# A rewritten opening and another order of products at chunk ends in a Fourier-mixing kernel with a gated feed-forward network

## The chip, the core and the metric

The kernel runs on one core of one Trainium2 chip. The core has five engines that run side by side, each working through its own list of instructions in order: TensorE (PE, matrix products; its weight loads are shown as PEld), VectorE (DVE), ScalarE (ACT), GpSimd (POOL) and SyncE (SP, which here only issues DMA transfers). They wait for each other through semaphores. The metric is the device time of one execution in microseconds; lower is better.

## The reference

`A_x` holds 8192 tokens of 448 numbers. Each token is normalised (`xn`, mean and variance over its 448 numbers). Two branches start from `xn` and meet at the end:

```python
xn = _layernorm(x, axis=-1)
s = _A_ref(xn, ...)          # rfft over the tokens, two complex block products
                             # (4 blocks of 112) with a relu between, soft threshold, irfft
g = _silu(_B_ref(xn, ...))   # (gelu(xn @ w_gate) * (xn @ w_up)) @ w_down, 448 -> 1792 -> 448
return x + s * g
```

Everything the change touches lies in the B branch, in the normalisation and in the first stage of the Fourier transform of the first tokens.

## The kernel before, in words

**Numbers.** Products are made in float16 pairs: a float32 operand is split into a high and a low float16 part, and three products (high by high, low by high, high by low) stand for one. So every weight and every token has a high and a low part to be made: ACT makes the high part (a cast or a scaled copy), DVE or POOL subtracts it from the original for the low one. Weights are first scaled by a power of two that comes from the largest magnitude in a block. That maximum is taken in three steps (`largest`, L442): DVE reduces along the rows, PE turns the column of maxima into a row by a product with a float32 identity (`identf`), DVE reduces again, PE spreads the result over all partitions, and DVE makes the scales (`scales`, L648).

**Tiling.** Tokens are taken as 64 tiles of 128 (4 tiles a chunk, 16 chunks; chunks 0 and 1 are special). The 1792 columns of the hidden layer are 14 blocks of 128, called f. The first pass (p=0) does f=0 to 7 for all chunks and stores partial sums; the second pass (p=1) does f=8 to 13, adds the partial sums, applies the silu, multiplies by the Fourier branch and stores the output. Chunks 0 and 1 of the first pass use plain products (`plain`, L1153): for each f, 22 matmuls of 512 columns, of gate and up together (for chunk 0, f=0 alone, they are done in two halves of 256 columns, tiles 0 and 2 first, then 1 and 3). From chunk 2 on, pairs of tiles and pairs of blocks are multiplied by a scheme with seven products in place of eight (`unit`, L1025, products 1 to 7 named a1 to a7), with combinations of weights (`gu_comb`, L731) and of tokens prepared beforehand. The token combinations are written to DRAM (`xts`) and read back transposed into `xta` and `xtb` (`xt_load`, L976).

**Phases.** Phase 1 normalises the tokens chunk by chunk and runs the first Fourier stage (`stage1`, L565); phase 2 does the block products of the Fourier branch; phase 3 the last Fourier stage. They are laid beside the feed-forward products, which run on PE from beginning to end.

**Order.** The order of instructions on each engine is made when the program is built, by a planner (`Pace`, L49). It keeps a planned time for every engine, ring buffer and DMA. Each part of the work is a Python generator; `yield` hands control to whichever task is due next, `yield ev(...)` waits in planned time for another task's `done(...)`. Operations are appended to their engine's list in the order in which the planner reaches them. On the chip there is no planner: the engines run their lists and wait on semaphores only for real data. Starts of later phases are tied to fixed planned times (`T1`, `DT`, `END1` to `END3`). `Either` (L204, called `B`) gives an operation to DVE or POOL, whichever ends first by plan. All instructions of the helper carry line L199 in the profile, so tiles tell them apart: `x` and `st` (tokens, statistics), `xs` (their float16 parts), `xta` (the transposed tokens of chunk 0, later the transposed combinations), `wst` (raw gate and up weights), `wt` (their float16 parts), `fx`, `fh`, `fe`, `fc` (maxima and scales), `dw` (down weights), `bx`, `by`, `bd`, `bf` (PSUM banks, two each).

**The opening** (`begin`, L1915) is written out by hand. It issues the loads of the four tiles of chunk 0 on SP's queue and of the first weight block and the identity on ACT's. Tile 0's mean and variance are made by DVE, those of tiles 2, 1 and 3 by ACT with two accumulating passes. POOL takes the power -0.5 and DVE refines it in four small operations (`rsqrt`, L518). DVE normalises (`normal`), ACT casts the high part, POOL (tile 0) or DVE (tile 2) subtracts for the low part, PE transposes both (`turn`, L1883), and DVE and ACT copy the transposed parts out of PSUM into `xta`. Then the first half of f=0 can start. Tiles 1 and 3 go the same way behind it (`token`, L1890), and stage 1 of all four tiles after that. `weights` (L2050) meanwhile starts the loads of the next blocks, `gu_block` (L662) takes their maxima and scales, and `gu_split` (L712) makes their parts; four buffers `wst` hold raw blocks. `down_weights` (L754) takes the maxima of the down weights, `begin1` (L2024) does the statistics and tokens of chunk 1, `gu_combs` (L700) the combinations for chunks 2 and on.

**A chunk end in the first pass** (`chunk`, L1441): after the last unit's products a3 and a7, the down products (`down`, L1364; for one tile 8 blocks x 3 matmuls of 448 columns) are made in the order tile 0 (f=0 to 5), the unit's last product a4, tile 1 (f=0 to 5), tile 0 and tile 1 (f=6, 7), tile 2, tile 3. Then the next chunk starts with its a1.

Of the kernel before, what the change touches and what calls it, by code (L numbers as in the profile page):

```python
# [24 lines left out]
PL = 2  # L25
# [23 lines left out]
class Pace:  # L49
# [4 lines left out]
    def __init__(self):  # L54
        self.now, self.last, self.n, self.heap = 0.0, 0.0, 0, []
        self.free, self.seen, self.dma = {}, {}, 0.0
        self.port = {"DVE": [], "POOL": []}
# [74 lines left out]
    def issue(self, e, op, out, ins, run):  # L132
        outs, ins, start = self.start(e, out, ins)
        if e == "SP":
# [33 lines left out]
    def cost(self, e, op, start, out, ins):  # L168
# [8 lines left out]
        if e == "POOL":  # L177
            t = 1.1 if n < 8 and op == "tensor_tensor_pow" else 0.2 + 0.0023 * n
        elif n < 32:
            return 0.17  # L180
        elif psum or sb < 2 and op != "tensor_scalar":
            return 0.14 + 0.00107 * (n + 60 * (extra > 0))
# [191 lines left out]
def afno_geglu_kernel(ctx, tc, x, gu, wd, mlp, b1, b2, c_m, c_mt, c_small, out):  # L374
# [81 lines left out]

    EV = {}
# [46 lines left out]
    def stats(c):  # L504
# [157 lines left out]
    def gu_block(b, to):  # L662

        f0, n = BLK[b]
        for i in range(n):
            yield ev("wl", f0 + i, 0)
            t = EV["wst", f0 + i, 0]
            V.tensor_reduce(fm[:, i, :, b], t[:, 0:8].rearrange("p (i k) f -> p i (k f)", i=2),
                            axis=AXIS.X, op=ALU.max, apply_absolute_value=True)
            yield  # L670
        mx = fx[:, :, b]
        if n == 2:
            V.tensor_tensor(mx, fm[:, 0, :, b], fm[:, 1, :, b], op=ALU.max)
        else:
            V.tensor_copy(mx, fm[:, 0, :, b])
        yield
# [3 lines left out]
        scales_of_products(b, to)  # L680
        done("scales", b)
        for i in range(n):
# [7 lines left out]
            done("w", f)  # L690
# [9 lines left out]
    def gu_combs(fs):  # L700
# [3 lines left out]
        for f in fs:  # L704
            yield ev("wl", f, 1)
            yield from gu_comb(f, EV["wst", f, 1], wt[f][:, :, 8:16])
# [5 lines left out]
    def gu_split(f, t, d, k):  # L712
        if 0 < f < PF[0][1]:
# [4 lines left out]
            yield  # L718
# [6 lines left out]
        yield  # L725
        V.scalar_tensor_tensor(d[:, 1, 0:4 - k], t[:, k:4], scale(f, 0), d[:, 0, 0:4 - k],
# [4 lines left out]
    def gu_comb(f, t, d):  # L731

        c = yield from CB.get()
# [16 lines left out]
        CB.put(c)  # L750
# [3 lines left out]
    def down_weights(p):  # L754
# [398 lines left out]
    def plain(c, f):  # L1153
# [5 lines left out]
        for q, tk in enumerate((slice(0, 256), slice(256, 512)) if (c, f) == (0, 0) else (slice(0, 512),)):  # L1159
# [3 lines left out]
            for p, v in ((u, 0), (g, 4)):  # L1163
                for t in range(3):
                    T.matmul(p[:, tk], w[:, 0, v + t], xT[t][:, tk], start=t == 0 and tk.start == 0, stop=False,
                             skip_group_check=True)
                    T.matmul(p[:, tk], w[:, 0, v + t], xT[4 + t][:, tk], start=False, stop=False,
                             skip_group_check=True)
                    T.matmul(p[:, tk], w[:, 1, v + t], xT[t][:, tk], start=False, stop=False,
                             skip_group_check=True)  # L1170
                    yield pe()
                T.matmul(p[:, tk], w[:, 0, v + 3], xT[3][:, tk], start=False, stop=False, skip_group_check=True)
                T.matmul(p[:, tk], w[:, 1, v + 3], xT[3][:, tk], start=False, stop=tk.stop == 512,
                         skip_group_check=True)
# [218 lines left out]
    def ffn():  # L1393
# [34 lines left out]
        rings = (BD, BD, BX, BX)  # L1428
# [11 lines left out]

    def chunk(p, i):  # L1441
# [9 lines left out]
        yield ev("xt", "a", p, i)  # L1451
# [9 lines left out]
        yield from units[0][0]()  # L1461
        yield pe()
# [43 lines left out]
        yield from down(p, i, 1, 0, cut, hv)  # L1506
        yield pe()
        for a in (0, 1):
            yield from down(p, i, a, cut, nf, hv)
            yield pe()  # L1510
        for a in (2, 3):
            yield from down(p, i, a, 0, nf, hv)
            yield pe()
        HT.put(h)
# [375 lines left out]
    def token(c, a, xs):  # L1890

        cast(c, a, xs)
        yield
        low(B, c, a, xs)
# [12 lines left out]
        for dst, src in parts:  # L1907
            if a in (0, 2):
# [6 lines left out]
    def begin():  # L1915
# [8 lines left out]
        for _ in range(2):  # L1924
            xss.append((yield from XS.get()))
        S.dma_start(w[:, 0:8 * 128], gu[0][:, 0:8 * 128])
# [196 lines left out]
```

## Time and profile before

| | us |
|---|---|
| median of 3 runs | 1806.65 (1806.02 to 1807.02) |
| the profiled execution | 1806.45 |
| its span, first to last instruction | 1804.6 |
| DVE, ACT, POOL busy | 1339.9, 997.5, 401.6 |
| first real product on PE | 14.14 after the span's start |
| f=1 starts on PE | 29.81 |
| chunk 0's last plain product | 76.90 |

The profile's page lists busy times, DMA queues and groups of instructions. Its other views are a table of busy time in chosen windows (each row: from and to, length, then busy time and count of instructions of PE, PEld, DVE, ACT and POOL, the granted clock of PE as a share of full speed, the DMA engines' busy share and GB/s), the list of waits (who waited for whom: us in total, times, longest), the timeline (start, duration, engine, line, operation, output tile <- input tiles, shapes, how many in a row, and in brackets the idle time before it and what ended it), and the view of one tile (per operation: shortest, median and longest duration in ns, first and last start).

### The profile page before, as it was taken

Reading aid. Unit: us, or ns where it says so; the run is one execution under the profiler, and the core shown is the slowest. Engines: PE = TensorE matmul, PEld = TensorE weight load, DVE = VectorE, ACT = ScalarE, POOL = GpSimd, SP = SyncE. Lnnn points to the kernel's source line nnn. Section 1 sums busy time; section 2 is a strip of 40 time slices with the busy share of each in tenths; the row PEclk is TensorE's granted clock in tenths of the full one; section 3 lists DMA queues with packets and bytes.
Section 4 is the critical chain, followed back from the end, with each engine's and each line's share of the span. In section 5 each row is a group of like instructions: output and inputs, shape, how many; then the busy total and the mean of one; then the engine's idle time right before and its main releaser. Section 6 shows DMA issues by size and latency. Waiting matters only on the chain. (4 is left out here: it accounts for less than half of the span.)

```text
span 1804.6 us, 38978 instructions
## 1 busy us (share of the span) xinstructions
PE 1769.2 (98%) x15725; PEld 1430.9 (79%) x15725; DVE 1339.9 (74%) x2441; ACT 997.5 (55%) x1911; POOL 401.6 (22%) x502
## 2 busy tenths in 40 slices
PE   7999999999999999999999999999999999999997
PEld 3447777767787777787887899999999998888886
DVE  7867778776865555656756788888888887888876
ACT  5736555555544444456666766767766763333333
POOL 3332333331221122100000222222221331222220
PEclk9999999999999999999999999999999999999999
DMA  6454576568455533332336634434344439899961
GB/s 218 158 153 157 161 193 201 186 183 233 140 144 167 135 111 94 89 70 76 78 105 182 149 103 120 120 89 109 87 115 120 111 72 268 261 312 303 298 219 52
DMA packets 345733, 277.03 MB, mean 154 GB/s; under 512 B 231536, under 2 KB 316784, under 8 KB 345552
## 3 DMA queue, kind: packets, MB, share of 16 engines
q1 hardware_dynamic: 345264, 273.98, 54.0%
q8 instruction: 123, 2.02, 0.5%
q10 hardware_dynamic: 288, 0.56, 0.1%
q14 instruction: 58, 0.48, 0.1%
HBM read 123.31 MB, written 102.02 MB: 125 GB/s over the span
## 5 line engine op out<-in xcount | busy, mean ns | idle before, releaser
L199 PEld LDWEIGHTS <-wt 128*128 128x128 f16 x9350 | 908.9, 98 | 176.7 <-issue 22.8
L199 PE MATMUL bx<-xta,wt 128*128 128x256 f16 (+1 forms) x3843 | 475.7, 275 | 0.8 <-ACT by L199 0.3
L199 PEld LDWEIGHTS <-h 128*128 128x128 f16 x2704 | 259.8, 98 | 128.2 <-issue 2.4
L199 PE MATMUL bd<-dw,h 128*128 128x448 f16 (+1 forms) x1920 | 344.6, 329 | 0.8 <-DVE pt L199 0.6
L199 PE MATMUL by<-xtb,wt 128*128 128x256 f16 x2080 | 249.9, 272 | 0.7 <-DVE by L199 0.7
L199 PE MATMUL by<-xta,wt 128*128 128x256 f16 (+1 forms) x1347 | 178.2, 282 | 4.5 <-DVE xta L199 3.1
L199 DVE TENSOR_TENSOR by<-bx,u 128x512 f32<-128x512 f32 x104 | 72.3, 695 | 95.3 <-PE bx L199 81.5
L199 POOL TENSOR_TENSOR wt<-wt 128x256 f32<-128x256 f32 x78 | 61.2, 785 | 355.1 <-DVE wt L199 337.5
L199 PE MATMUL bx<-xtb,wt 128*128 128x256 f16 x1040 | 130.5, 272 | 2.8 <-DVE v L199 2.4
L199 ACT COPY u<-by 128x512 f32<-128x512 f32 x104 | 60.7, 584 | 88.0 <-PE by L199 87.9
L199 ACT ACTIVATE u<-by,fc 128x512 f32<-128x512 f32 (+1 forms) x118 | 73.6, 636 | 49.1 <-PE by L199 48.8
L199 PE MATMUL bd<-dw,wt 128*128 128x224 f16 (+1 forms) x816 | 93.8, 264 | 5.6 <-DVE pt L199 5.4
L199 ACT CAST h<-wt 128x512 f16<-128x512 f32 (+1 forms) x128 | 68.6, 536 | 46.1 <-DVE wt L199 39.9
L199 DVE SCALAR_TENSOR_TENSOR pt<-bd,fb,pt 128x448 f32<-128x448 f32 x96 | 64.6, 680 | 28.4 <-PE bd L199 27.7
L199 ACT ACTIVATE th<-bd,fb 128x448 f32<-128x448 f32 x62 | 39.1, 632 | 83.5 <-PE bd L199 74.8
L199 PE MATMUL bf<-w2t,wn 112*128 112x112 f16 x1512 | 84.9, 213 | 0.0
L199 DVE TENSOR_TENSOR v<-bx,u 128x512 f32<-128x512 f32 x104 | 71.1, 684 | 16.5 <-PE bx L199 16.1
L199 PEld LDWEIGHTS <-wn 112*128 112x128 f16 x1512 | 80.5, 98 | 2.0
L199 DVE SCALAR_TENSOR_TENSOR u<-by,fc,u 128x512 f32<-128x512 f32 (+1 forms) x86 | 55.5, 659 | 33.2 <-PE by L199 20.4
L199 ACT ACTIVATE gl<-bx,fc 128x512 f32<-128x512 f32 (+1 forms) x70 | 40.5, 599 | 71.0 <-PE bx L199 69.4
L199 ACT COPY by<-bx 128x512 f32<-128x512 f32 x104 | 59.9, 576 | 35.5 <-PE bx L199 35.3
L199 ACT ACTIVATE th<-pt 128x448 f32<-128x448 f32 x64 | 37.1, 580 | 72.0 <-DVE pt L199 65.4
(215 smaller groups left out, 2901.3 us busy)
## 6 DMA issues: line engine op xcount, KB each, us to landing
xts<-sx SPq DMA_DIRECT2D x32, 480.0 KB, 3.0
x<-in_x SPq DMA_DIRECT2D x17, 896.0 KB, 6.3
t<-ysb SPq DMA_DIRECT2D x64, 224.0 KB, 3.2
prt<-th SPq DMA_DIRECT2D x64, 224.0 KB, 2.1
pt<-prt SPq DMA_DIRECT2D x64, 224.0 KB, 3.8
u<-t SPq DMA_DIRECT2D x32, 448.0 KB, 6.2
x<-in_x SPq DMA_DIRECT2D x32, 448.0 KB, 6.9
y<-t SPq DMA_DIRECT2D x30, 448.0 KB, 3.7
```

Source lines behind the costliest of these rows:

```text
L199: return self.pace.issue(self.name, kind, out, ins, lambda: fn(out, *args, **kw))
```

## The change

It rewrites the opening, changes when the planner lets the preparation of weights go ahead, and changes the order of products at the ends of chunks in the first pass.

- **Planner.** Engines start at planned times of 0.7 to 1.0 us in place of 0; a DMA issued by ACT, POOL's small power and DVE's copies of float16 from PSUM get other planned costs. These alter orders, not operations.
- **Dummy matmuls.** `keep(n, w)` issues n matmuls of w columns on a tile of ones, into a bank that the first stage-1 product overwrites later: 14 of 512 columns at the very start, 2 and 4 of 256 between the first small matmuls and transposes. Their results are not used.
- **Statistics.** Tiles 0 and 3 by DVE, 2 and 1 by ACT; POOL takes the power and also the four refining operations. ACT makes `identf`.
- **Order in `begin`.** Tiles 1 and 3 are normalised and cast before the low parts of f=0's weights are made; stage 1 of tiles 0 and 2 moves between the first transposes and the products; the maximum of weight block 1 is taken inside `begin`.
- **Weights.** From block 2 on, a maximum waits (in planned time) for the scales of the block before and for a lull on DVE; a block is announced as ready (`done("w", f)`) after its first high half; statistics of chunk 1 wait for the maxima of block 3 and for a lull, and the maxima of the down weights for the last of the eight weight blocks. Combinations of odd f take another buffer, so two can be under way.
- **`plain`.** All products with the high part of the weights come before those with the low part.
- **Chunk ends.** The order becomes tile 0 (f=0 to 5), a4, tile 0 (f=6, 7), tile 2, tile 1, then the next chunk's a1 (if by plan its transposed tile has landed), then tile 3. Chunk 1's down products take the banks bx before bd.

The diff, cut to its core:

```diff
+        self.free, self.seen, self.dma = {"SP": 0.7, "ACT": 0.7, "DVE": 0.7, "POOL": 0.7, "PE": 1.0}, {}, 2.8
...
+    def lull(e):
+        while pace.free.get(e, 0.0) > pace.now + 0.05:
+            yield pace.free[e]
...
         for a in range(CH):
+            if c < PL:
+                yield from lull("DVE")
             V.bn_stats(s6[:, a, :], x4[:, a, :])
...
             yield ev("wl", f0 + i, 0)
+            if to == 0 and b > 1:
+                yield ev("scales", b - 1)
+                yield from lull("DVE")
+            if to == 0 and b == 1:
+                continue
...
+            e = pace.spawn(gu_comb(f, EV["wst", f, 1], wt[f][:, :, 8:16]))
+            yield ev("taken", f)
+        yield e
...
-        if 0 < f < PF[0][1]:
+        if 1 < f < PF[0][1]:
             for i in range(2):
                 w = t[:, 4 * i:4 * i + 4]
                 S.activation(w, w, AF.Copy, scale=scale(f, i))
                 S.copy(d[:, 0, 4 * i:4 * i + 4], w)
-            yield
+                yield
+                if i == 0:
+                    done("w", f)
...
+        done("w", f)
+        if f == 1:
+            yield ev("max", 2)
...
+            if p == 0:
+                yield ev("w", PF[0][1] - 1)
             for i in range(n):
+                if p == 0:
+                    yield from lull("DVE")
                 V.tensor_reduce(dmx[:, f + i:f + i + 1], v[:, i], axis=AXIS.X, op=ALU.max, apply_absolute_value=True)
...
+            for s, seq in ((0, (0, 4, 1, 5, 2, 6, 3)), (1, range(4))):
+                for p, v in ((u, 0), (g, 4)):
+                    for k, x in enumerate(seq):
+                        add(p, s, v + x % 4, x, 7 * s + k)
...
-        rings = (BD, BD, BX, BX)
+        rings = (BX, BX, BD, BD)
...
-        yield from down(p, i, 1, 0, cut, hv)
+        yield from down(p, i, 0, cut, nf, hv)
         yield pe()
-        for a in (0, 1):
-            yield from down(p, i, a, cut, nf, hv)
-            yield pe()
-        for a in (2, 3):
+        for a in (2, 1):
             yield from down(p, i, a, 0, nf, hv)
             yield pe()
+        if nxt[0] == 0 and ev("xt", "a", *nxt).done:
+            state["ahead"] = unit(0, nxt[1], 0, Later(), EV["xta", 0, nxt[1]])
+            yield from state["ahead"][0]()
+            yield pe()
+        yield from down(p, i, 3, 0, nf, hv)
+        yield pe()
```

and of `begin`, the new order of operations:

```diff
+        keep(14, 512)
         S.activation(fb[:, 4:5], mhalf[:, 0:1], AF.Gelu_apprx_tanh)
+        S.copy(identf, ident)
...
+        def root(i, n):
+            v = rs[:, i:i + n]
+            G.tensor_tensor(v[:, :, 1], v[:, :, 0], mhalf[:, 0:n], op=ALU.pow)
+            rsqrt(G, v)
...
+        moments(0)
+        variance(0)
+        root(0, 1)
+        sums(2)
+        squares(2)
         V.tensor_reduce(mx, t[:, 0:8].rearrange("p (i k) f -> p i (k f)", i=2), axis=AXIS.X, op=ALU.max,
                         apply_absolute_value=True)
+        variance(2)
+        root(1, 1)
+        normal(0)
+        sums(1)
+        squares(1)
         big = banks[2]
         T.matmul(big[0:2, 0:128], mx, identf, start=True, stop=True)
+        keep(2, 256)
...
+        moments(3)
+        cast(0, 0, xss[0])
         turn(banks[0], 0, xss[0], 0)
+        keep(4, 256)
         normal(2)
+        low(G, 0, 0, xss[0])
+        variance(1)
+        variance(3)
+        root(2, 2)
         cast(0, 2, xss[1])
...
         V.tensor_copy(xT[:, :, 0:128], turned(banks[0]))
         BF.put(banks[0])
+        V.tensor_reduce(fx[:, :, 1], EV["wst", 1, 0][:, 0:8].rearrange("p (i k) f -> p i (k f)", i=2), axis=AXIS.X,
+                        op=ALU.max, apply_absolute_value=True)
         turn(banks[1], 2, xss[1], 1)
+        stage1_at(0, first[0])
+        S.activation(d[:, 0, 4:8], t[:, 4:8], AF.Copy, scale=scale(0, 1))
         S.copy(xT[:, :, 128:256], turned(banks[1]))
...
+        normal(1)
+        cast(0, 1, xss[0])
+        normal(3)
+        cast(0, 3, xss[1])
+        tasks = [pace.spawn(token(0, a, xss[a // 2], *e), pace.free["DVE"]) for a, e in ((1, (G, V)), (3, (V, V)))]
         V.scalar_tensor_tensor(d[:, 1, 0:4], t[:, 0:4], scale(0, 0), d[:, 0, 0:4], op0=ALU.mult, op1=ALU.subtract)
         V.scalar_tensor_tensor(d[:, 1, 4:8], t[:, 4:8], scale(0, 1), d[:, 0, 4:8], op0=ALU.mult, op1=ALU.subtract)
```

More of the change, by code (lines that the diff above doesn't have):

```diff
@@ L1460, in chunk @@
         units = [unit(p, i, f0, h, xa) for f0 in range(0, nf, 2)]
[L1461 to L1462 removed]
+        if "ahead" in state:
+            units[0] = state.pop("ahead")
+        else:
+            yield from units[0][0]()
+            yield pe()
         prev = None
@@ L2007, in begin @@
         done("wl", 1, 0)
-        yield pace.free["POOL"]
-        rsqrt(V, rs[:, 1:4:2])
-        tasks = []
-        for a in (1, 3):
-            normal(a)
-            tasks.append(pace.spawn(token(0, a, xss[a // 2]), pace.last))
-            yield
+        yield at + 1.0
+        stage1_at(2, first[1])
+        scales_of_products(0, 0)
+        scale_of_gate(0)
+        rests = [leave1(a, b) for a, b in ((0, first[0]), (2, first[1]))]
+        yield
+        rests[0]()
+        BX.put(first[0])
+        yield ev("scales", 1)
+        rests[1]()
+        BY.put(first[1])
         for e in tasks:
             yield e
+        GL.put(gl)
         X4.put(x4)
```

185 lines of the change are left out of this document (111 added, 74 removed).

## Prediction

> **What bounds the kernel now.** I read the page's engine line first, then the busy time by stage, then who TensorE (PE) waited for.
>
> ```profile
> PE 1769.2 (98%) x15725; PEld 1430.9 (79%) x15725; DVE 1339.9 (74%) x2441; ACT 997.5 (55%) x1911; POOL 401.6 (22%) x502
> ```
>
> ```profile
> core 0: us, PE busy (x) PEld busy (x) DVE busy (x) ACT busy (x) POOL busy (x), PEclk, DMA share, GB/s
> 0.00:14.14 14.14, 4.02 (x20) 2.15 (x21) 8.23 (x25) 8.43 (x20) 2.45 (x8) 1.00 0.85 317
> 14.14:29.81 15.67, 12.47 (x71) 7.87 (x71) 10.48 (x26) 5.62 (x15) 4.04 (x4) 0.89 0.35 115
> 29.81:76.90 47.09, 44.61 (x219) 20.37 (x219) 41.43 (x99) 35.60 (x71) 18.54 (x20) 0.96 0.53 172
> 76.90:996.00 919.10, 915.60 (x7284) 678.84 (x7283) 623.25 (x1165) 489.15 (x905) 188.15 (x268) 1.00 0.51 143
> 996.00:1797.00 801.00, 792.55 (x8136) 721.64 (x8133) 652.38 (x1123) 458.12 (x902) 188.39 (x203) 1.00 0.59 163
> ```
>
> ```profile
> PE bd L199 <- DVE fx L199: 7.7, 1, 7.7
> PE bd L199 <- DVE pt L199: 6.0, 16, 1.2
> PE by L199 <- DVE xta L199: 3.1, 1, 3.1
> PE bf L199 <- DVE fx L199: 2.5, 1, 2.5
> ```
>
> PE is busy 98% of the span, so nothing but PE's idle time and its slow clock can be won. The windows (cut at the first real product, the start of the second weight block f=1, the end of token chunk 0, the end of the first pass) show where that lies. Before 14.14 us PE has 4.02 us of work. In the second window it idles 15.67-12.47 = 3.20 us, in the third 47.09-44.61 = 2.48 us. From 76.9 to 996 us it idles 3.50 us in all, from 996 to 1797 us 8.45 us. The three single long waits (7.7, 3.1, 2.5 us) are all in the opening, and all wait for VectorE (DVE).
>
> ```profile
> 14.14 2.51 PE L199 MATMUL by<-xta,wt 128*128 128x256 f16 x11 [0.99 <-ACT xta L199]
> 16.44 2.33 PE L199 MATMUL bx<-xta,wt 128*128 128x256 f16 x11
> ...
> 24.45 0.49 PE L199 MATMUL by<-xta,wt 128*128 128x256 f16 x3 [3.05 <-DVE xta L199]
> ...
> 29.81 0.82 PE L199 MATMUL by<-xta,wt 128*128 128x512 f16 x3
> ...
> 77.12 2.54 PE L199 MATMUL by<-wt,wt 128*128 128x512 f16 x11
> ```
>
> The clock costs too. Late in the opening eleven 512-column matmuls take 2.54 us with the last one's drain, about 0.22 us each, so 256 columns should take about 0.11. At 14.14 eleven matmuls of 256 columns take 16.44-14.14 = 2.30 us, 0.21 each: half speed, although the clock column reads 1.00 there (its records evidently begin later). That is 22 x 0.10 = 2.2 us lost. The clock of 0.89 takes (1-0.89) x 15.67 = 1.7 us more from the second window, 0.96 takes 1.9 us from the third. So 3.2+2.2+1.7 = 7.1 us can go in the second window, 2.5+1.9 = 4.4 us in the third.
>
> **The change, part by part.** *Up to the first product.* The four loads of x keep their order on SyncE's queue, the first gu block and the identity stay on ScalarE's (ACT's) queue; issue and landing cost nothing new. The 14 dummy matmuls run while PE waits 7.7 us for DVE anyway: at half speed 14 x 0.42 = 5.9 us, free as long as they start before about 1.5 us; if they start later, the first small matmul slips by as much. The tail of tile 0 and tile 2 decides the start:
>
> ```profile
> 7.93 0.56 POOL L199 TENSOR_TENSOR st<-st,mhalf 128x1 f32<-128x1 f32 x1 [0.78 <-DVE st L199]
> 9.79 1.03 POOL L199 TENSOR_TENSOR xs<-x,xs 128x448 f16<-128x448 f32 x1 [1.29 <-ACT xs L199]
> ...
> 42.10 0.20 POOL L199 TENSOR_SCALAR st<-st 128x4 f32<-128x4 f32 x1
> 42.38 0.20 POOL L199 TENSOR_TENSOR st<-st 128x4 f32<-128x4 f32 x1
> ```
>
> ```profile
> 9.94 1.13 DVE L199 TENSOR_SCALAR x<-x,st 128x448 f32<-128x448 f32 x1
> ...
> 11.70 0.62 DVE L199 TENSOR_TENSOR xs<-x,xs 128x448 f16<-128x448 f32 x1
> 12.24 0.62 DVE L199 COPY xta<-bf 128x896 f16<-128x896 f16 x1
> ```
>
> ```profile
> 13.18 0.91 ACT L199 COPY xta<-bf 128x896 f16<-128x896 f16 x1 [0.27 <-PE bf L199]
> ```
>
> GpSimd (POOL) now does the whole root, four small operations 42.38-42.10 = 0.28 us apart, 1.1 us a tile. Tile 0's four push tile 2's power from 7.93 to about 8.5; with 0.56 and 1.1 us tile 2's scale is there near 10.3, where the old normalisation began at 9.94. It was then held to 1.13 us by POOL's 1.03 us subtraction, and in the new order that subtraction stands right behind the root, so the two still meet. I put tile 2, and with it ACT's copy at 13.18, 0.5 us later: first product at 14.7. (Bounds: 0.5 us earlier if they don't meet, since DVE is rid of the small operations; 1.5 us later if POOL's chain slips.) Two stage-1 products move ahead, in time PE spends waiting.
>
> *Second half of chunk 0 (tiles 1 and 3).* Now PE waits until 24.45 for DVE:
>
> ```profile
> 20.99 0.62 DVE L199 COPY xta<-bd 128x896 f16<-128x896 f16 x1
> 21.53 2.33 DVE L199 TENSOR_REDUCE fm<-wst 128x2 f32<-128x1024 f32 x2
> 23.78 0.61 DVE L199 COPY xta<-bd 128x896 f16<-128x896 f16 x1
> ```
>
> The last copy stands behind 2.33 us of maxima for later weights. These are now held back, and the statistics of tiles 1 and 3 come early. Adding up DVE's new order: first copy done at 12.24+0.5+0.6 = 13.3; one maximum (2.33/2) 14.5; two normalisations at 0.5, 15.5; two low parts of the weights at 0.7, 16.9, or 17.9 if POOL's subtraction of tile 1 (1.03 us) blocks them as it did at 9.94; tile 3's subtraction 0.62, 18.5; transposes 0.5; two copies 1.2: about 20.3. So 24.45 becomes 20.3. The first half itself is no limit: from 14.7, 4.6 us at half speed, and the low-part products now come last, when their weights (17.9) are there.
>
> *f=1.* After the second half comes 22 x 0.11 = 2.4 us (4.6 at half speed), with some 0.8 us of small matmuls: f=1 at 23.5 (bounds 21 and 26). Its maximum is taken by 14.5, its scale by about 20, its high part by 22. Gain 29.81-23.5 = **6.3 us**.
>
> *f=2 to 7.* PE consumes a block of two f in 2 x 22 x 0.22 = 9.7 us.
>
> ```profile
> 30.39 0.16 DVE L199 TENSOR_SCALAR fe<-fx 128x2 int32<-128x2 int32 x1
> ...
> 44.24 0.16 DVE L199 TENSOR_SCALAR fe<-fx 128x2 int32<-128x2 int32 x1
> ```
>
> These rows close the scales of blocks 2 and 3: 13.85 us apart, slower than PE eats, which made the 2.48 us gap. DVE was then doing chunk 1's statistics and the maxima of w_down. The change puts both behind the weights in DVE's order, announces a block after its first high half, and runs 14 high products (3 us) before the first low part is needed. The new waits are the planner's: on the chip they mean later places in the engines' orders, and what is put back is wanted late (w_down's at the down products, which now start at 117.37). Of the 4.4 us I let 1.1 remain as new small waits: **3.3 us**. Bounds: all of 4.4, or 3 us of new waits. Three stage-1 matmuls that used to run here have moved ahead into idle time: 3 x 0.19 = **0.6 us**.
>
> *Combinations, planner's costs.* Odd blocks use a second buffer; the combined weights are wanted only after chunk 1's down products, so I cost this at nothing; without cover a late block is a wait of some 5 us once. The planner's new costs change order alone.
>
> *Chunk ends, first pass.*
>
> ```profile
> 117.37 18.32 PE L199 MATMUL bd<-dw,h 128*128 128x448 f16 x96
> ```
>
> ```profile
> DMA to landing us min/median/max: 6.2/7.9/11.1
> ```
>
> All matmuls stay, in another order; 13 times the next chunk's first 12 products come before the last down product. They need the next transposed tile, whose load is issued when the last product that reads the old one is done. Between lie 18+6+24+24 = 72 matmuls of 448 columns at 18.32/96 = 0.19 and ten of 256: 13.7+1.1 = 14.8 us, against landings of 6.2 to 11.1. So it hides. What can be won is inside the 3.50 us that PE idles from 76.9 to 996: the first copies of a chunk and ACT's drains of the accumulators get more cover; I take **1.0 us** (bounds: 3.5 gained, 2 lost).
>
> Sum: 6.3+3.3+0.6+1.0 = 11.2 us. All later work is the same, and PE is busy in it, so a head start reaches the end. The profiled execution took 1806.45 us (span 1804.6), 0.2 below the median: 1806.45-11.2 = 1795.25; against the median **1795.4 us**.
>
> [...]
>
> **The rivals.**
>
> *Weights still bound* (chance 0.20). If blocks keep coming 13.85 us apart, the chain from maximum to scale being PE and DVE in turn, PE waits at f=2, 4 and 6. With the first scale near 20 and f=1 at 23.5, f=6 starts near 62 instead of 52, and part of each wait takes up other matmuls: chunk 0 ends near 72 instead of 76.9, gain 4.9+1.0: 1800.5; with the clock shut after each gap, 1802. For it: DVE is busy 41.43 of 47.09 us. Against it: what slowed it then is moved back.
>
> *The clock stays open* (0.13). If the dummies hold it through the first products, 2.2 us more go, and 2.3 more if neither the POOL meeting nor the new waits come: 11.2+4.5 = 15.7, 1790.7.
>
> *Slower: the early product waits for its transposed tile* (0.06). If the landing came over 14.8 us after the last reader, PE would wait 13 times with the last down product queued behind. At 16.5 us: 13 x 1.7 = 22 us lost, 11.2-1.0 gained: 1818. It turns the sign above 14.8+10.2/13 = 15.6 us. Against it: the longest landing is 11.1. For it: SyncE's queue is in order, and a store ahead of the load can hold it.
>
> *No change* (0.06): the later passes are paced by fixed planned times, so the end could wait for them.
>
> ```profile
> L199 SPq DMA_DIRECT2D out<-g x20: 343/357/1420, 1511.1 to 1741.9; - x20
> ```
>
> Their last paced store is issued at 1741.9, 55 us before PE ends; against it. It would give 1806. That the dummies or the early product do nothing at all (the planner leaves the latter out when its tile is not yet landed by plan) costs at most 1 us and lies in the forecast.
>
> **How the numbers follow.** Forecast 0.55 (1791.5 to 1799), weights still bound 0.20, clock open 0.13, slower 0.06, no change 0.06. Range: the lower end takes f=1 at 21 (8.8), 4.4+0.6 and half the 3.5: 15.6, and 2 us of luck in the last pass's 8.45 us of waits, which shift anyway: 1789. The upper end takes f=1 at 26 (3.8) and nothing else: 1802.5. 0.2% (3.6 us) is about what a measurement of this kernel can tell from no change. Of rival one 0.01 lies within it. Faster: 0.55+0.13+0.19 = 0.87; same 0.06+0.01 = 0.07; slower 0.06.
>
> **What would show it.** Right: first 256-column product near 14.7, second half near 20, first 512-column product near 23.5, PE idle under 1.5 us from there to the end of chunk 0, that end near 66; the same 3.5 us or less of idle in the first pass. Wrong: scales of blocks still 13 us apart (rival one), 256-column products 0.11 us apart from the start (rival two), PE waits on xta at chunk ends (rival three), or idle PE near the end (rival four).

## The result and the profile after

The changed kernel takes 1806.58 us (median of 14 runs, 1805.39 to 1809.29), the kernel before 1806.56 us (14 runs beside them, 1803.87 to 1808.81): ratio 1.0002, 95% interval 0.9994 to 1.001. The change makes no difference that can be measured; forecast were 1795.4 us and a range from 1789 to 1802.5. The profiled execution took 1807.62 us, its span 1805.5.

The engine line of the page of the changed kernel, and its table of busy time in the same windows as before (columns as there):

```profile
PE 1775.5 (98%) x15745; PEld 1431.7 (79%) x15745; DVE 1339.4 (74%) x2414; ACT 991.1 (55%) x1905; POOL 420.7 (23%) x531
```

```profile
0.00:14.14 14.14, 10.27 (x40) 4.22 (x40) 6.52 (x15) 7.21 (x17) 6.38 (x25) 0.85 0.86 316
14.14:29.81 15.67, 14.87 (x96) 8.70 (x96) 13.86 (x27) 6.47 (x14) 1.24 (x1) 0.92 0.62 201
29.81:76.90 47.09, 43.79 (x210) 19.09 (x208) 37.43 (x79) 30.75 (x61) 11.49 (x13) 0.96 0.52 168
76.90:996.00 919.10, 914.00 (x7254) 678.03 (x7253) 624.78 (x1162) 488.11 (x906) 210.70 (x286) 1.00 0.50 142
996.00:1797.00 801.00, 792.33 (x8152) 721.70 (x8150) 651.83 (x1124) 457.95 (x907) 190.84 (x206) 1.00 0.58 163
```

In the second window PE's idle time has fallen from 3.20 to 15.67-14.87 = 0.80 us. But in the third it has grown from 2.48 to 47.09-43.79 = 3.30, and from 76.9 to 996 us from 3.50 to 919.10-914.00 = 5.10. The list of PE's waits in the changed kernel shows the same (us in total, times, longest):

```profile
PE bd L200 <- DVE pt L200: 4.5, 12, 1.2
PE bf L200 <- DVE k L200: 3.3, 5, 1.3
PE by L200 <- DVE by L200: 2.4, 2, 1.9
```

The three long waits of the opening are gone from the top of the list; in their place stand single waits of 1 to 2 us, nearly all for DVE, and spread over the whole run. PE's timeline in the opening, changed kernel:

```profile
15.63 0.59 PE L200 MATMUL bf<-identf,fx 128*2 128x128 f32 x2
16.15 1.14 PE L200 MATMUL by<-xta,wt 128*128 128x256 f16 x7
...
22.38 0.49 PE L200 MATMUL by<-xta,wt 128*128 128x256 f16 x3 [0.78 <-DVE xta L200]
...
25.91 0.81 PE L200 MATMUL by<-xta,wt 128*128 128x512 f16 x3
...
58.14 0.96 PE L200 MATMUL bd<-ident,xs 128*128 128x128 f16 x8 [0.58 <-POOL xs L200]
...
61.11 1.46 PE L200 MATMUL by<-xta,wt 128*128 128x512 f16 x3 [0.72 <-ACT wt L200]
```

The first product starts at 16.15 us (before 14.14), the second half at 22.38 (24.45), f=1 at 25.91 (29.81): 3.9 us gained. At 61.11 f=6 starts with a wait for its weights, after some 4 us in which PE had only transposes, maxima and one tile's stage-1 products left; behind that stretch the granted clock is 0.50, half speed, from 60.98 to 64.39, which makes the 0.96 of the third window.

**Where the time went.** For the whole run I compare *program points*: how much matmul work, at full clock, lies behind an instruction of PE (0.216, 0.189 and 0.109 us for each matmul of 512, 448 and 256 columns, their spacing in the kernel before from 77.12, 117.37 and 381.92 us on; smaller ones by their spacing; dummies not counted). P1 has 30 us of it behind it, P2 130 us (chunk 1's end), P3 1750 us; in kernels that leave work out or add some, P2 and P3 are counted from the end. The starts at these points, from the traces:

| | P1 | P2 | P3 | time lost from P2 to P3 |
|---|---|---|---|---|
| before | 55.9 | 157.7 | 1782.5 | 4.8 |
| changed | 47.7 | 154.1 | 1783.5 | 9.3 |

(P3 less P2 less 1620 us of work. How high the last column stands depends on what the small matmuls are counted at; the differences between its rows hardly do. Each trace is of one execution, and executions of one kernel differ by some 5 us.) The changed kernel is 8.2 us ahead at P1, 3.5 at P2, and 1.0 behind at P3. Two things are to be explained: 4.7 us lost before chunk 1's end, 4.5 us more lost in the 1620 us of work behind it, where the change alters nothing but the chunk ends.

### The profile page after: what moved, and what is told of

Read it like the earlier page. It is cut to its first block, busy times and chain, and to the rows that moved or that the text cites. A ratio compares the mean times of both kernels' runs of the same rounds, so it can differ in the third digit from the quotient of the medians.

```text
span 1805.5 us, 39001 instructions
## 1 busy us (share of the span) xinstructions
PE 1775.5 (98%) x15745; PEld 1431.7 (79%) x15745; DVE 1339.4 (74%) x2414; ACT 991.1 (55%) x1905; POOL 420.7 (23%) x531
## 3 DMA queue, kind: packets, MB, share of 16 engines
q8 instruction: 123, 2.02, 0.5%
## 5 line engine op out<-in xcount | busy, mean ns | idle before, releaser
L200 ACT COPY by<-bx 128x512 f32<-128x512 f32 x104 | 59.8, 575 | 55.9 <-PE bx L200 55.7
L200 POOL TENSOR_TENSOR zs<-t,zs 112x256 f16<-112x256 f32 (+1 forms) x35 | 30.1, 860 | 204.2 <-ACT zs L200 171.1
L200 PEld LDWEIGHTS <-w1t 112*112 112x112 f16 x612 | 68.2, 130 | 9.1 <-issue 4.1
```

The lines of the kernel that those rows point to most:

```text
L200: return self.pace.issue(self.name, kind, out, ins, lambda: fn(out, *args, **kw))
```

## Experiments

Four theories stood. (A) The wait put before the later maxima makes weight block 4 (f=6, 7) late, and that loses about 5 us of the opening. (B) Later passes are paced by fixed planned times and take any head start back. (C) The new chunk ends cost time of their own. (D) Placement: every edit makes the planner lay out all later work anew, and which background operation then stands ahead of an urgent one on DVE or ACT costs a different sum in each layout.

**Block 4 without its wait** (from the changed kernel; this drops both the wait for the scales of the block before and the lull):

```diff
-            if to == 0 and b > 1:
+            if to == 0 and 1 < b < 4:
```

> The changed kernel, but the maxima of weight block 4 (f=6, 7) no longer wait in planned time for the scales of block 3 and for a lull on DVE; blocks 2 and 3 still do. Theory A: the head start of the opening (8.2 us of lost PE time less, when 30 us of matmul work is done) is first lost at f=6, because block 4's scales come at 59.1 us. Then here they come before 54 us, the 3.4 us of half clock at 61 us go, chunk 0's last plain product ends near 68.5 in place of 73.1 and, if nothing else takes it, the time is 1802. Theory B (the later phases, tied to fixed planned times, take back whatever the opening gives): the same 68.5, but a time of 1806 to 1807. Theory C (the chunk ends cost 3 us): 1802 too, so it does not tell A from C.

1797.72 us, ratio to before 0.9967 (0.9955 to 0.998): faster than both kernels. (The median of the kernel before itself went from 1804.8 to 1806.6 us between sets of runs; kernels of different sets are compared by these ratios.) DVE's timeline of the changed kernel (first) and of this one (second) shows the first of block 4's two maxima (the reductions of `wst`) and the end of its scales (`fe`); the row at 39.37 ends block 3's:

```profile
39.37 0.16 DVE L200 TENSOR_SCALAR fe<-fx 128x2 int32<-128x2 int32 x1
...
48.64 1.21 DVE L200 TENSOR_REDUCE fm<-wst 128x2 f32<-128x1024 f32 x1
...
59.13 0.15 DVE L200 TENSOR_SCALAR fe<-fx 128x2 int32<-128x2 int32 x1
```

```profile
42.28 1.22 DVE L200 TENSOR_REDUCE fm<-wst 128x2 f32<-128x1024 f32 x1
...
53.16 0.16 DVE L200 TENSOR_SCALAR fe<-fx 128x2 int32<-128x2 int32 x1
```

The first maximum moves from 48.64 to 42.28 and the scales from 59.13 to 53.16; the half clock at 61 us is gone (granted clock 1.00 from 29.81 to 76.90), and P2 comes at 151.5 instead of 154.1. A stands as a mechanism, for 2.6 us at P2 where about 5 were expected. But at P3 the two traces are 10.0 us apart (1773.5 against 1783.5): behind P2 this kernel loses 2.0 us, the changed one 9.3.

**The new chunk ends alone** (the kernel before with the order of down products, the early a1 and the banks of the changed one):

```diff
-        rings = (BD, BD, BX, BX)
+        rings = (BX, BX, BD, BD)
...
-        for a in (2, 3):
+        for a in (2, 1):
```

> The kernel before with the new chunk ends alone (early a1, new order of down products, other order of banks for chunk 1). Theory C, the chunk ends cost what the opening gains: about 3 us slower, 1809.5, with new PE waits at chunk ends. Theory A, the chunk ends cost and bring next to nothing: 1805 to 1808, waits at chunk ends gone (some 0.5 us), the opening as before (f=1 at 29.8).

1810.24 us, 1.0032 (1.0019 to 1.0045). By itself that speaks for C. Yet the loss is mostly one wait near 390 us, from the list of PE's waits:

```profile
PE bf L199 <- DVE dmx L199: 4.8, 1, 4.8
```

`dmx` is a maximum of the later down weights, background work that now stands in PE's and DVE's order at a bad place. DVE's row shows that it is late because DVE itself stood idle until a load of these weights had landed:

```profile
384.97 1.80 DVE L199 TENSOR_REDUCE dmx<-wst 128x1 f32<-128x448 f32 x3 [16.16 <-DMA wst<-in_down]
```

Behind this wait, too, the products run at half speed: the next 20 of 256 columns take 4.34 us, some 2 us more than at 0.109 us each.

**The new opening alone** (the changed kernel with the old chunk ends and banks, the lines above reversed):

> The changed kernel with the chunk ends of the kernel before: the opening alone. Theory C: 3 us faster than both, 1803.5. Theory A: opening as in the changed kernel (f=1 at 25.9, chunk 0's end at 73), time 1804 to 1808 depending on which later waits the new order of instructions happens to make. Theory B: 1806.5.

1819.05 us, 1.0085 (1.0071 to 1.0099). With the new opening the old ends are *slower* than the new ones by 1.0085 against 1.0002, 15 us: C, as a cost of the ends' own, falls. The time is above what all three theories had allowed. P1 comes at 47.8 as in the changed kernel; behind P2 22.0 us are lost.

**Without the dummy matmuls** (the changed kernel less its three `keep` calls):

```diff
-        keep(14, 512)
...
-        keep(2, 256)
...
-        keep(4, 256)
```

> The changed kernel without the 20 dummy matmuls. If the clock they open (6.4 us) is shut again before the first product (the records of the changed kernel say shut at 9.8, open at 16.6), they bring nothing: first product within 0.5 us of 16.2, the clock open at 16 to 20 us, time within 1.5 us of 1806.6. If they do hold the clock, the first half of f=0 takes 2 us longer and the time is 1808.5.

1807.33 us, 1.0013 (1.0004 to 1.0022); P1 at 48.3 instead of 47.7. The dummies are worth 0.6 us at P1 and nothing that can be told apart at the end.

**The planner's costs alone** (the kernel before with only the planner's new starts and costs; each operation stays, but 14 go to DVE instead of POOL):

```diff
-        self.free, self.seen, self.dma = {}, {}, 0.0
+        self.free, self.seen, self.dma = {"SP": 0.7, "ACT": 0.7, "DVE": 0.7, "POOL": 0.7, "PE": 1.0}, {}, 2.8
...
-            t = 1.1 if n < 8 and op == "tensor_tensor_pow" else 0.2 + 0.0023 * n
+            t = 0.7 if n < 8 and op == "tensor_tensor_pow" else 0.2 + 0.0023 * n
...
```

> The kernel before with the planner's new start times and costs alone: no operation added or taken away, only orders planned anew. Theory D (placement: the later hundreds of us are planned anew by any edit, and which background operation happens to stand ahead of an urgent one on DVE or ACT is worth several us either way): opening within 1 us of before, lost PE time between 130 and 1400 us different by 2 us or more, total off by 2 to 10 us in either direction. Theory C (the edits' own direct cost): within 1.5 us of before, 1803.5 to 1806.5 beside a before of 1805.

1821.08 us, 1.0081 (1.0066 to 1.0096). An edit that I had priced at nothing ("change order alone") costs 15 us, more than D had allowed (2 to 10). P2 is at 158.3, 0.6 us late; 18.2 us are lost behind it, against 4.8 in the kernel before. Its longest single wait behind P2 is one of PE for ACT, 3.7 us at 393 us.

**The planned start of the later stages moved by 3** (`T1`, planned time only), in the kernel before and in the changed one:

```diff
-    T1, DT = 84.0, 42.0
+    T1, DT = 87.0, 42.0
```

> The kernel before with the background work of the first pass (normalising and combining chunks 2 to 17) planned 3 us later (87 in place of 84), nothing else. Theory D: 2 to 10 us off in either direction, the difference arising in waits on DVE and ACT between 130 and 700 us. Theory C: within 1.5 us, as 3 us later is nothing against landings that have over 10 us to spare.

> The changed kernel with the same background work planned 3 us earlier (81), so that it follows the head start that the opening still has at chunk 0's end (3 us). Theory B (fixed planned times take the head start back): the alignment of the kernel before is restored, the later waits shrink, 1803.5. Theory D: off by 2 to 10 us in either direction, with waits in other places. If neither, 1806 to 1807.5.

The kernel before at 87: 1809.78 us, 1.0024 (1.0015 to 1.0034); some 3 us more is what fixed pacing would give too. The changed kernel at 81: 1816.3 us, 1.0055 (1.004 to 1.007), where fixed pacing asks for about 3 us less than 1806.6. B falls, and the kernel before at 81 (below) is slower too, where it should be faster.

**Block 4 without its wait, old chunk ends:**

> The version with block 4's maxima set free, with the chunk ends of the kernel before. The opening alone was 12 us slower with old ends than with new ones, with waits of up to 1.9 us at chunk ends and starts (PE for ACT and DVE) between 155 and 275 us. If the new ends are what protects against these, they come back: 1803 to 1812, in place of 1797.7. If the loss was one unlucky placement (theory D alone), it need not return: 1795 to 1800.

1812.75 us, 1.0038 (1.0023 to 1.0053), against 0.9967 with the new ends: 13 us. P2 is at 153.0; 15.3 us are lost behind it.

**The other planned starts**, so that each of three kernels stands at three of them:

> The version without the wait in planned time for weight blocks 4 and 6 took 1797.72 us. Here its fixed planned start of the later stages is moved from 84 to 81; no operation changes. If its 9 us come from the opening (a robust gain), the time stays within 3 us of 1797.7. If they are for a good part a lucky placement of background operations on DVE and ACT (the changed kernel and the kernel before lost 9.7 and 3.2 us by like moves), it comes out at 1800 to 1813, with new single waits of PE for ACT or DVE of 1 to 4 us after 100 us, and the first 60 us alike.

> The same with the planned start at 87. Robust gain: within 3 us of 1797.7. Lucky placement: 1800 to 1813, and not the same as with 81.

> The changed kernel with the planned start at 87 (81 gave 1816.3). If the end is set by where background operations fall, this is a third draw: 1803 to 1820, with the first 60 us as in the changed kernel. If the later stages' fixed planned times paced the end, it would be 3 us above 1806.6, as 81 should have been 3 us below.

> The kernel before with the planned start at 81 (87 gave 1809.8). Placement: 1808 to 1822, since its waits between 77 and 1750 us are few and a re-plan can mostly add. Fixed pacing: 1803.6. With the other three it gives each of three kernels at three planned starts, so that what the edit does can be set against what a move of the plan does.

Ratios to the kernel before, as it is, with their intervals:

| planned start | 81 | 84 (as is) | 87 |
|---|---|---|---|
| before | 1.0024 (1.0014 to 1.0033) | 1 | 1.0024 (1.0015 to 1.0034) |
| changed | 1.0055 (1.004 to 1.007) | 1.0002 (0.9994 to 1.001) | 1.0024 (1.0014 to 1.0034) |
| block 4 without its wait | 0.9997 (0.9988 to 1.0006) | 0.9967 (0.9955 to 0.998) | 1.0015 (1.0005 to 1.0024) |

A move of 3 in the plan changes the time by 0.2 to 0.5%, as much as the edits that are to be judged. The 0.33% of the first experiment are in good part a lucky layout: at 81 and 87 nothing is left against the kernel before as it is. Against the kernel before at the same start, the version without the wait is ahead by 0.27, 0.33 and 0.09%, and the changed kernel behind by 0.31, 0.02 and 0%. The first is clear of the intervals at two starts and within them at 87; its size is not known.

All these versions changed the plan. What was open was whether later stages absorb a head start by themselves or the new layout takes it. The last four separate the two.

**A head start with every order held.** In the kernel before, 36 matmuls of chunk 1 are left out on the chip, and the planner counts them all the same; DVE, ACT, POOL and SP then have the same lists, instruction by instruction. With `n = 2` they are doubled instead. The third kernel does the same to the changed one; the fourth is the first with the planner told.

```diff
+        def low(out, *ins, **kw):
+            n = 0 if c == 1 and 1 <= f < 7 else 1
+            pace.issue("PE", "matmul", out, list(ins), lambda: [T.engine.matmul(out, *ins, **kw) for _ in range(n)])
...
-                    T.matmul(p[:, tk], w[:, 1, v + t], xT[t][:, tk], start=False, stop=False,
+                    low(p[:, tk], w[:, 1, v + t], xT[t][:, tk], start=False, stop=False,
```

> The kernel before, with 36 matmuls of chunk 1 left out on the chip (for f=1 to 6, tokens' high part by weights' low part), while the planner still counts them: the order of every engine's other instructions is the same, instruction by instruction. This is a head start of 36 x 0.216 = 7.8 us at about 80 to 117 us and nothing else. If a head start reaches the end when the order stands still (the prediction's step, and the re-plan is what takes the gain), 1806.0 - 7.8 = 1798.2 within 2 us. If later stages (background work on DVE and ACT, fixed times) absorb a head start by themselves, 1802 to 1806.

> The same 36 products issued twice, the planner counting them once: same order, PE 7.8 us later. Carried to the end: 1813.8 within 2 us. Absorbed by slack: 1806 to 1810.

> The changed kernel with the same 36 products left out on the chip and counted by the planner; its order stands still. Carried: 1806.6 - 7.8 = 1798.8 within 2 us. Absorbed: 1803 to 1807.

> The kernel before with the same 36 products left out and the planner told so: the same head start, but the order of all later work is made anew (409 differing lines in DVE's list of 2303). If re-planning is what costs: above 1798.2, 1800 to 1813, with single waits of PE for DVE or ACT of 1 to 4 us that the version with the order held does not have. If re-planning is harmless: as the version with the order held, within 2 us.

| | time, us | ratio to before | P2 | P3 | lost from P2 to P3 |
|---|---|---|---|---|---|
| before | 1805.32 | 1 | 157.7 | 1782.5 | 4.8 |
| before, 36 less, order held | 1800.75 | 0.9971 (0.9959 to 0.9982) | 153.1 | 1776.4 | 3.3 |
| before, 36 more, order held | 1813.42 | 1.0038 (1.0025 to 1.0051) | 164.5 | 1788.0 | 3.5 |
| before, 36 less, planned anew | 1805.0 | 0.9999 (0.999 to 1.0008) | 149.6 | 1780.8 | 11.2 |
| changed | 1806.58 | 1.0002 (0.9994 to 1.001) | 154.1 | 1783.5 | 9.3 |
| changed, 36 less, order held | 1808.84 | 1.0019 (1.0009 to 1.0028) | 153.7 | 1784.3 | 10.6 |

(Times and ratios from several runs, the points from the profiled one; the two rows before and changed for comparison, the points of the first from its earlier trace, the latter with its own set's ratio.) This is the answer. In the kernel before with its order held, what is won or lost at P2 reaches the end: 4.6 us at P2 give 4.6 us in the time, 6.8 us of delay give 8.1. And the time lost behind P2 belongs to the layout: 3.3 to 4.8 us in the order of the kernel before, whether early or late, 9.3 to 10.6 in that of the changed one (and some 10.7 in the version without the dummies, whose lists on DVE, ACT, POOL and SP are the changed kernel's, too). The one planned anew is 8.1 us ahead at P2, more than with the order held, and loses 11.2 behind it: nothing is left. My two bare alternatives (carried whole, or absorbed) missed both kernels with 36 less, since a held order also hinders PE at the very place where it gets early: of 7.8 us left out in chunk 1, the order of the kernel before kept 4.6 at P2, that of the changed kernel 0.4 (and its ratio is 0.17% above the changed kernel's).

PE's single waits say the same, from the timelines. Between 150 and 1750 us these are all over 0.9 us:

| order of the other engines | traces | waits, us (place) |
|---|---|---|
| before | before; 36 less; 36 more | 0.91 (355); 0.91 (351); 0.91 (362) |
| changed | changed; without dummies; 36 less | 1.95, 2.39, 2.36 (384); 1.29, 2.02, 2.02 (400); 1.35, 1.35, 1.19 (694); 0.94, 0.95, 0.94 (1043); 1.27, 1.27, 1.27 (1094) |
| planned anew | before, 36 less, planned anew | 1.57 (180); 1.62 (309); 1.64 (382); 1.44 (386); 1.00 (487) |

The same products wait in every trace of one order, and others in another order: this is no accident of single executions. In all, PE is idle 9.8 us from 130 to 1790 us before and 12.2 in the changed kernel, and the half clock at 385 us takes 1.7 more: together 4.1 of the 4.5 us.

Why the head start in chunk 1 was not kept, the windows show (77 to 120 us: before, changed, changed with 36 less):

```profile
77.00:120.00 43.00, 43.00 (x204) 19.74 (x203) 30.99 (x54) 21.68 (x35) 14.32 (x23) 1.00 0.53 158
```

```profile
77.00:120.00 43.00, 43.00 (x205) 19.88 (x205) 40.03 (x77) 25.97 (x43) 24.62 (x34) 1.00 0.32 98
```

```profile
77.00:120.00 43.00, 37.15 (x167) 16.68 (x166) 39.93 (x79) 25.71 (x43) 24.11 (x35) 0.92 0.37 115
```

DVE, 30.99 us busy there before, is now 40.03 of 43 us busy, in part with work that the change put back out of the opening (the low parts of the down weights). PE does not wait for it yet, but it cannot be much earlier either. The granted clock is lower in the last row as well: 0.92, which is (1-0.92) x 43 = 3.4 us more. DVE's timeline, and the row of PE that waits for it, in the third kernel:

```profile
96.59 1.31 DVE L200 TENSOR_SCALAR x<-x,st 128x448 f32<-128x448 f32 x2 [0.67 <-POOL st L200]
97.82 0.41 DVE L200 TENSOR_TENSOR cb<-wst,cb 128x256 f32<-128x256 f32 x1
98.16 1.62 DVE L200 SCALAR_TENSOR_TENSOR wt<-wo,fc,wt 128x1024 f16<-128x1024 f32 x1
99.70 0.94 DVE L200 TENSOR_TENSOR sf<-x 128x256 f32<-128x256 f32 x1
100.56 0.74 DVE L200 SCALAR_TENSOR_TENSOR u<-by,fc,u 128x512 f32<-128x512 f32 x1
...
101.36 1.86 PE L200 MATMUL by<-wt,wt 128*128 128x512 f16 x4 [4.41 <-DVE u L200]
```

To move on PE needs only the last of these DVE lines, the drain of `by` at 100.56; four lines of background work (normalisation, combinations of weights, a Fourier operand) stand ahead of it.

The same can be read far behind, in the kernel planned anew (timeline of ACT, DVE and PE):

```profile
382.21 0.58 ACT L199 COPY u<-by 128x512 f32<-128x512 f32 x1
382.21 0.61 DVE L199 BATCH_NORM_STATS2 st<-x 128x6 f32<-128x448 f32 x1
...
384.41 0.59 DVE L199 BATCH_NORM_STATS2 st<-x 128x6 f32<-128x448 f32 x1
...
385.14 0.68 DVE L199 TENSOR_TENSOR by<-bx,u 128x512 f32<-128x512 f32 x1
...
385.87 0.60 PE L199 MATMUL by<-xtb,wt 128*128 128x256 f16 x4 [1.44 <-DVE by L199]
```

ACT has `u` ready at 382.79, but DVE takes four tiles' statistics (first and last shown), background work for a later chunk, before the addition for which PE waits. With the order held, the same addition comes soon after its input is there (before, 36 less, order held):

```profile
380.20 0.59 ACT L199 COPY u<-by 128x512 f32<-128x512 f32 x1
...
381.03 1.08 DVE L199 TENSOR_TENSOR wo<-cb,wo 128x896 f16<-128x896 f32 x1
...
382.03 0.69 DVE L199 TENSOR_TENSOR by<-bx,u 128x512 f32<-128x512 f32 x1
...
382.78 1.25 PE L199 MATMUL by<-xtb,wt 128*128 128x256 f16 x10 [0.22 <-DVE by L199]
```

Here the rest of one operation and another of 1.08 us stand between, and PE waits 0.22 us.

## Why the prediction was wrong

*Dummies: right.* They start at 1.44 us, just inside the bound of 1.5, and their removal costs nothing measurable. The granted clock of the changed kernel around the first products (its table of windows):

```profile
6.40:9.78 3.38, 1.77 (x10) 0.66 (x9) 2.33 (x5) 3.16 (x11) 2.65 (x10) 1.00 1.04 394
9.78:16.60 6.82, 5.99 (x28) 2.58 (x29) 5.19 (x12) 3.32 (x6) 3.37 (x11) 0.50 0.59 236
16.60:29.81 13.21, 12.43 (x89) 7.93 (x87) 11.40 (x23) 4.97 (x12) 1.24 (x1) 1.00 0.74 238
```

It is 1.00 from 6.40 to 9.78, 0.50 from 9.78 to 16.60, where PE was busy 5.99 of 6.82 us with transposes, small products and four dummies, and 1.00 again 0.45 us behind the start of the first product at 16.15. The sign that I gave for the rival *the clock stays open*, 256-column products 0.11 us apart, came true for all but the first 0.45 us, without its gain: the sum had the first half at half speed, yet the second half still came late.

*First product 14.7: came at 16.15*, at the far end of the stated bound (1.5 us later). The meeting of POOL's subtraction and DVE's normalisation that I forecast is there (POOL and DVE of the changed kernel):

```profile
10.33 1.03 POOL L200 TENSOR_TENSOR xs<-x,xs 128x448 f16<-128x448 f32 x1
...
10.42 1.20 DVE L200 TENSOR_SCALAR x<-x,st 128x448 f32<-128x448 f32 x1 [0.61 <-POOL st L200]
```

The same operation of DVE took 0.51 us at 54.67, when POOL was idle. After that, ACT's transposed copy began at 14.41, 1.2 us later than before where I had put 0.5, and not counted was the maxima matmul of block 1 that now stands ahead of the product on PE (15.63 in the timeline above).

*Second half 20.3: 22.38; f=1 at 23.5: 25.91, inside its bounds of 21 and 26.* The mechanism held and the size was off: 3.9 us instead of **6.3**. The term that was too small is the end of DVE's list: before the two copies stand block 1's scales, which wait for PE's maxima matmul, and the copies begin at 21.18 (DVE of the changed kernel):

```profile
20.63 0.16 DVE L200 TENSOR_SCALAR fx<-bf 128x2 f32<-128x2 f32 x1 [0.81 <-PE bf L200]
...
21.18 1.15 DVE L200 COPY xta<-bd 128x896 f16<-128x896 f16 x2
```

*f=2 to 7, **3.3** + 0.6: failed.* Between f=1 and P1 the changed kernel did gain, to 8.2 us ahead. Then the wait before block 4's maxima gave it back: chunk 0 ends at 73.1 instead of 76.9, 3.8 us gained, so that f=2 to 7 brought 3.8-3.9 = -0.1 us. The step that failed is "Of the 4.4 us I let 1.1 remain as new small waits": in the third window 3.30 us of idle PE and 1.7 us of half clock remained, 5.0. I had written that the new waits mean later places in the engines' orders, but followed only the operations put back, and not the one kind of urgent operation that the same wait puts back, the maxima of the next blocks. The first experiment shows it. The rival *weights still bound* came closest here: it had f=6 near 62 and chunk 0's end near 72, and they came at 61.11 and 73.1. Its mechanism was only half right, since the blocks do not keep coming late one after the other: blocks 1 to 3 close their scales at 21.11, 30.98 and 39.37, block 4 alone at 59.13. Its time, 1800.5, failed with the head start that it too carried to the end.

*Combinations "at nothing"* held as far as PE does not wait for them in the changed kernel; but they are among the work that leaves DVE no room in chunk 1 (97.82 and 98.16 above).

*Chunk ends 1.0:* cannot be told by themselves. With the old opening the new ends cost 0.32%, with the new opening they save 0.83, with block 4 freed 0.71. Each is one layout against another. That the early product waits for its transposed tile did not happen: no wait of PE for `xta` behind the opening is in the list of the changed kernel.

*"All later work is the same, and PE is busy in it, so a head start reaches the end": failed.* The second half is true of the kernel before, as its held order shows. The first half is false for this kernel: the operations are the same, their order isn't. The layout behind P2, with the new chunk ends in it, takes 9.3-4.8 = 4.5 us, more than the 3.5 us that the changed kernel is ahead there. Summed up: 11.2 forecast; f=1 short by 2.4, f=2 to 7 by 4.0, the layout 4.5; the chunk ends and 0.3 us between chunk 0's end and P2 make up the rest to 1.0 us behind in the profiled pair, and nothing in the medians.

The rival *no change* gave the right time for a wrong reason (pacing by fixed planned times: at 81 the changed kernel is 10 us slower, not 3 faster). A rival "the plan is made anew and costs as much" was missing, though the kernel's own description named the planner as the maker of all orders.

Open: what makes one layout cheap (2.0 us lost behind P2) and another dear (22.0) was read for single waits only, not derived; whether the lull alone or also the wait for the scales delays block 4 was not tried; and which part of the new order causes the five waits in the table above was not isolated. Nor is it known how often a newly planned order is dear: only the few layouts above were tried.

## What to carry to other kernels

Where a static planner lays out the whole program, judge an edit with the order of all other work held, or over several layouts (a planned time moved by a little): here one layout against the next was worth up to 15 us, the change's own head start 3.5 at P2. In an opening, ask of every wait not only what it puts back but whether something urgent stands behind the same wait, and where the work put back will land; an engine at 40 of 43 us there left no room for PE to be early. Look for the loss behind the place of the edit: a ladder of equal program points shows where two traces part.

## What the runs showed of the hardware

In the changed kernel 3.41 us at half clock stand behind a wait of 1.95 us, which ends at 384 us (PE's timeline, then the windows around it):

```profile
384.19 1.31 PE L200 MATMUL by<-xtb,wt 128*128 128x256 f16 x10 [1.95 <-DVE by L200]
385.30 4.43 PE L200 MATMUL bx<-xta,wt 128*128 128x256 f16 x24
```

```profile
381.83:385.24 3.41, 1.47 (x14) 1.16 (x13) 3.34 (x7) 1.33 (x4) 0.00 (x0) 1.00 1.00 317
385.24:388.65 3.41, 3.41 (x18) 2.38 (x17) 1.93 (x6) 0.49 (x2) 1.23 (x2) 0.50 1.01 392
```

PE was busy 1.47 of 3.41 us, and the 24 products behind it took 4.43 us. With the planned start at 81, the changed kernel has the same products, nearly the same wait, and the 24 products take 2.78 us:

```profile
390.65 1.25 PE L200 MATMUL by<-xtb,wt 128*128 128x256 f16 x10 [1.93 <-DVE by L200]
391.74 2.78 PE L200 MATMUL bx<-xta,wt 128*128 128x256 f16 x24
```

```profile
388.00:391.41 3.41, 1.48 (x14) 1.17 (x13) 2.53 (x6) 0.84 (x2) 2.14 (x3) 1.00 0.73 282
```

So the half clock cost 4.43-2.78 = 1.65 us here beyond the wait itself; it came behind a window in which PE was busy 1.47 us, and not behind this one with 1.48. In the traces of the kernel before and the changed one, each recorded stretch at one granted clock, save the last, is a whole multiple of 3.41 us long: half clock from 25.24 to 28.65 and 49.13 to 52.54 us before, from 9.78 to 16.60, 60.98 to 64.39 and 385.24 to 388.65 in the changed kernel. Cut into windows of 3.41 us on that grid, from 19 us to 15 us before the end, the two traces have four that are followed by half clock, with PE busy 0.79 and 1.04 us (before), 2.15 and 1.47 us (changed); the least busy of the others have 2.50 (before) and 2.06 us (changed). So none of the four was idle throughout, and half clock followed one with PE busy 2.15 us where it did not follow one with 2.06.

A two-column operation of DVE, 0.17 us for block 3's scales, took 1.08 us for block 4's, while POOL worked on 512 columns, and both ended at 59.2 us (changed kernel, POOL, then DVE):

```profile
58.05 1.15 POOL L200 TENSOR_TENSOR h<-u,h 128x512 f16<-128x512 f32 x1
```

```profile
39.30 0.17 DVE L200 TENSOR_SCALAR fc<-fh 128x2 f32<-128x2 f32 x1
...
58.14 1.08 DVE L200 TENSOR_SCALAR fc<-fh 128x2 f32<-128x2 f32 x1
```
